# Attention in front of a routed network: a new plan for the steps of 16 units, taken by four engines in the order issued

## The chip, the cores and the metric

The kernel runs on one core of one Trainium2 chip. The metric is the device time of one execution, in microseconds (us), smaller is better. The kernel was timed in three runs; one further execution was recorded by the profiler.

## What is computed

Three networks follow each other: attention with packed queries, a layer of eight experts to which tokens are given by capacity, and a dense network. The change lies in the attention.

```
batch, n_heads, seq, head_dim = (8, 8, 576, 64)
n_pack = 32
...
def sm_attn(qq, kk, vv):
    s = scale * np.matmul(qq, kk.transpose(0, 1, 3, 2))
    s = s - np.max(s, axis=-1, keepdims=True)
    a = np.exp(s)
    a = a / (np.sum(a, axis=-1, keepdims=True) + 1e-09)
    return np.matmul(a, vv)
p_packed = sm_attn(p, k, v)
out = sm_attn(q, p_packed, p_packed)
...
x = np.ascontiguousarray(attn_out.transpose(0, 2, 1, 3)).reshape(B * S, H * D)
x = _moe_ref(x=x, **moe_kwargs)
return _moe2_ref(x=x, **moe2_kwargs)
```

First the 32 packed queries `p` of a head attend to its 576 keys and values (`p_packed`, 32 x 64), then the 576 queries `q` attend to the 32 rows of `p_packed`. The result `x` (4608 tokens x 512) goes through a gate (`x @ w_gate`), by which the experts take their tokens.

## The kernel before

The engines are TensorE (PE, its weight loads PEld), VectorE (DVE), ScalarE (ACT), GpSimd (POOL) and SyncE (SP), which issues the loads. The attention is cut into 16 units, each of four heads of one batch entry. The class `Attention` has one function for each step of a unit `u`:

- `s1_mm` (L112, PE): scores of the packed queries against the keys `kt`, into a PSUM tile `big`. `s1_max` (L118, L119, DVE): their maximum, and it times -0.125. `s1_exp` (L123, ACT): the exponential into `A`, with its sum.
- `s1_turn` (L130, PE): five transposes of `A` into another `big`. `s1_keep` (L136, L137, ACT): they are copied to `AT`. `pk_mm` (L145, PE): the product with the values `vt`, `ve`, into the one small PSUM tile `sm`.
- `pk_keep` (L151, L152, L154, DVE): one over the sum, scale and mask, into `pp`. `pk_turn` (L161, PE): two transposes into `sm`. `pk_keep2` (L167, DVE): two copies to `ppT`.
- `s2_mm` (L174, L178, PE): the product with the gate weights and the scores of the queries `qt`, into a third `big`. `s2_turn` (L184, L185, DVE): the scores turned in blocks of 32 into `w`, and the gate part copied to `Z`.
- `s2_max` (L189, DVE): row maximum. `s2_sub` (L215, POOL, three pieces): subtracted from `w`. `s2_exp` (L197, ACT): exponential of `w`. `s2_sum` (L201 to L203, DVE): row sum and its inverse. `s2_div` (L215, POOL, three pieces): `w` times the inverse. For the last unit both are one instruction on DVE (L211).
- `s2_back` (L219, DVE): `w` turned back into `A2`. `logits` (L226, PE): the unit's part of the gate logits, added up in the PSUM tile `LE` over all units.

`PLAN` gives each step a time in units, and `all_units` issues all steps of all units by the sum of the unit's number and that time:

```
def all_units(self):
    for _, u, n in sorted((u + t, u, n) for u in range(NU) for n, t in PLAN):
        getattr(self, n)(u)
```

In the kernel before, this is only the order of the program. What an engine takes first is settled by the framework's scheduler, which may put one step ahead of another on the same engine. Only from the routing on does PE have its order written out (`manual_schedule` with PE alone).

The PSUM tiles `big` are three buffers, which go round in the order of the program; `sm` is one. The loads `kt`, `vt`, `ve` and `qt` have four buffers each, and SP issues them in a fixed order (`setup`, L73 to L104): the keys and values of a unit, then the queries of the unit before. A load waits until its buffer is free.

When the last unit's logits are in `LE`, `take` copies it (L306, DVE), `load` turns it and the routing begins (L313 on). Products of `x_rows` (`px`, L242 on PE, copied to `xt` by ACT in L245, sent off by SP) make the tokens `x` from `A2` and `pp`; the first of them stand between the last logits on PE, the others between the steps of the routing.

Of the kernel before, what the change touches and what calls it, by code (L numbers as in the profile page):

```python
# [44 lines left out]
def wait(k, n):  # L45
# [1 line left out]

PLAN = [('s1_mm', 0), ('s1_max', 0.25), ('s1_exp', 1.06), ('s1_turn', 1.1), ('s1_keep', 1.5), ('pk_mm', 1.51),  # L50
        ('pk_keep', 1.7), ('pk_turn', 1.95), ('pk_keep2', 1.96), ('s2_mm', 2.25), ('s2_turn', 2.55),
        ('s2_max', 3.5), ('s2_sub', 3.65), ('s2_exp', 3.8), ('s2_sum', 3.81), ('s2_div', 4.57),
        ('s2_back', 6.15), ('logits', 6.7)]

TINY = float(np.uint32(0x380FFFFF).view(np.float32))

# [1 line left out]
class Attention:  # L58
# [172 lines left out]
# [3 lines that stand above are left out]
# [591 lines left out]
def fused_kernel(ctx: ExitStack, tc: tile.TileContext, a: dict, out: bass.AP):  # L825
# [20 lines left out]
    att = Attention(tc, a, ident, LE, xd)  # L846
# [1 line left out]
              pool(s_att, "ps_big", 3, space=PSUM), pool(s_att, "ps_sm", 1, space=PSUM))  # L848
    att.xpool = xpool
    rt = Routing(tc, a, rconst, rwk, ident, idx_all)  # L850
    att.all_units()
    le = rt.take(LE[0:96, 0:384])
    s_att.close()

# [136 lines left out]
```

## Time and profile before

| | us |
|---|---|
| median of three runs | 1525.36 (1525.34 to 1527.59) |
| the profiled execution | 1521.4 |
| span of its trace, from the first to the last instruction | 1519.4 |
| PE busy | 1436.2 (95% of the span) |
| DVE busy | 838.5 (55%) |
| ACT busy | 781.7 (51%) |
| POOL busy | 183.2 (12%) |
| mean granted clock of PE | 0.982 of full speed |

The profiled execution's time is 2.0 us more than its span. Times in the rows below are in us from the start of the span. A busy share is an average over parts of the program with quite different limits: the attention has the first 130 us or so, the routing and the experts follow, then the dense network. Matmuls are pipelined, and their ends are modelled.

### The profile page before, as it was taken

What the parts mean: (1) busy time and instruction counts of PE and PEld (TensorE: products, weight loads), DVE (VectorE), ACT (ScalarE), POOL (GpSimd) and SP (SyncE); (2) the same over time, 40 slices, a digit from 0 to 9 for tenths busy, and PEclk for the clock granted to TensorE, in tenths of its full rate; (3) what the DMA queues carried; (4) which work ended last, traced back from release to release, by engine and by line L of the source; (5) the groups of instructions that cost most, each with busy time, mean ns of one, the idle gap of its engine ahead of it and who ended that gap; (6) DMA issues with size and microseconds to landing.
All of it is one profiled execution on the core that took longest, in us unless ns stands there. A gap on an engine that the chain in (4) does not pass through costs nothing.

```text
span 1519.4 us, 22513 instructions
## 1 busy us (share of the span) xinstructions
PE 1436.2 (95%) x9009; PEld 1183.9 (78%) x9009; DVE 838.5 (55%) x1779; ACT 781.7 (51%) x966; POOL 183.2 (12%) x269
## 2 busy tenths in 40 slices
PE   6878699999999999999999999999999999999997
PEld 3335478888889899999788888888888888888885
DVE  4775588777778677543344454544445444454443
ACT  2333444433435344444656566565665656666564
POOL 2441301011010103032601010100101010010101
PEclk9999899999999999999999999999999999999999
DMA  9843636363645548452410020201002020100000
GB/s 339 304 143 126 223 131 220 120 217 127 216 141 190 171 143 307 158 179 93 158 56 28 0 83 1 83 0 56 28 1 83 1 76 7 56 28 0 28 0 28
DMA packets 66840, 165.36 MB, mean 109 GB/s; under 512 B 8880, under 2 KB 21808, under 8 KB 66736
## 3 DMA queue, kind: packets, MB, share of 16 engines
q1 hardware_dynamic: 60656, 144.00, 27.9%
q0 software_dynamic: 6080, 19.93, 3.8%
q8 instruction: 71, 1.16, 0.3%
q14 instruction: 33, 0.27, 0.1%
HBM read 117.76 MB, written 46.14 MB: 108 GB/s over the span
## 4 chain that ended last, share of the span: by engine, by line
issue 49%; PE 24%; DVE 5%; DMA 4%; POOL 3%; ACT 2%; SPq 0%; POOLq 0%; DVEq 0%; ACTq 0%
PE pm L624 18%; PE ph L624 3%; PE po L794 2%; DMA raw<-in_w 2%; POOL out L804 2%; DMA raw<-wd 2%; DVE w L547 1%; POOL w L547 1%; ACT w L540 1%; PE pt L693 1%; DVE h L715 1%; DMA xg<-xd,idx 0%; DVE dbig L585 0%; PE pr L379 0%; DVE xl L696 0%
## 5 line engine op out<-in xcount | busy, mean ns | idle before, releaser
L624 PE MATMUL ph<-y,w 128*128 128x512 f32 x1728 | 414.9, 395 | 0.0
L794 PE MATMUL po<-w,g 128*128 128x512 f32 x1728 | 410.1, 394 | 0.9 <-ACT g L769 0.9
L624 PEld LDWEIGHTS ph<-y,w 128*128 128x128 f32 x1728 | 324.1, 188 | 78.2
L794 PEld LDWEIGHTS po<-w,g 128*128 128x128 f32 x1728 | 324.9, 188 | 75.4 <-ACT g L769 1.7
L769 ACT ACTIVATE u<-u 128x1024 f32<-128x1024 f32 (+1 forms) x219 | 229.4, 1049 | 193.5 <-DVE u L773 183.2
L624 PE MATMUL pm<-h,w 128*128 128x288 f32 x1536 | 235.1, 303 | 1.8 <-DVE h L715 1.6
L624 PE MATMUL pm<-xh,w 128*128 128x288 f32 x1024 | 219.3, 304 | 0.7 <-ACT xh L695 0.7
L624 PEld LDWEIGHTS pm<-h,w 128*128 128x128 f32 x1536 | 209.7, 189 | 9.6 <-issue 3.1
L773 DVE TENSOR_SCALAR u<-ph 128x1024 f32<-128x1024 f32 (+1 forms) x73 | 88.2, 1209 | 200.4 <-PE ph L624 200.4
L769 ACT ACT_TABLE_LOAD x144 | 184.8, 1283 | 2.6
L776 DVE TENSOR_TENSOR u<-ph,u 128x1024 f32<-128x1024 f32 (+1 forms) x73 | 88.2, 1209 | 172.5 <-ACT u L769 172.5
L624 PEld LDWEIGHTS pm<-xh,w 128*128 128x128 f32 x1024 | 169.2, 192 | 8.2 <-issue 4.8
L624 PE MATMUL pm<-xl,w 128*128 128x288 f32 x512 | 156.2, 305 | 0.3 <-DVE xl L696 0.2
L778 DVE TENSOR_TENSOR u<-ph,u 128x1024 f32<-128x1024 f32 (+1 forms) x73 | 88.1, 1208 | 73.3 <-ACT u L769 73.3
L769 ACT ACTIVATE g<-u 128x1024 fp32r<-128x1024 f32 (+1 forms) x73 | 76.4, 1048 | 101.3 <-DVE u L778 93.8
L540 ACT ACTIVATE w<-raw 128x1024 fp32r<-128x1024 f32 x80 | 84.4, 1058 | 80.9 <-DMA raw<-in_w 60.6
L804 POOL DMA_INDIRECT out<-ot,idx_all x36 | 35.0, 971 | 726.8 <-DVE ot L802 721.0
L624 PEld LDWEIGHTS pm<-xl,w 128*128 128x128 f32 x512 | 98.3, 192 | 6.5 <-issue 4.4
L714 ACT ACTIVATE h<-pm 128x288 fp32r<-128x288 f32 x128 | 50.9, 405 | 90.4 <-PE pm L624 89.1
L780 DVE TENSOR_TENSOR g<-u,g 128x1024 fp32r<-128x1024 f32 (+1 forms) x73 | 88.2, 1209 | 2.7 <-ACT g L769 2.7
L683 POOL DMA_INDIRECT xg<-xd,idx x40 | 42.2, 1054 | 367.7 <-PE pr L395 186.8
L715 DVE SCALAR_TENSOR_TENSOR h<-pm,h 128x288 fp32r<-128x288 f32 x128 | 57.0, 451 | 51.2 <-ACT h L714 50.1
(160 smaller groups left out, 1133.5 us busy)
## 6 DMA issues: line engine op xcount, KB each, us to landing
raw<-in_w SPq DMA_DIRECT2D x64, 512.0 KB, 4.7
yd<-y SPq DMA_DIRECT2D x64, 288.0 KB, 3.3
kt<-in_k SPq DMA_DIRECT2D x16, 576.0 KB, 9.5
qt<-in_q SPq DMA_DIRECT2D x16, 576.0 KB, 8.8
vt<-in_v SPq DMA_DIRECT2D x16, 512.0 KB, 7.3
xd<-xt SPq DMA_DIRECT2D x32, 256.0 KB, 2.0
draw<-in_win SPq DMA_DIRECT2D x16, 512.0 KB, 4.3
wd<-dbig SPq DMA_DIRECT2D x32, 256.0 KB, 2.9
```

Source lines behind the costliest of these rows:

```text
L540: self.nc.scalar.activation(w[:, 0].rearrange("p a b -> p (a b)"), raw, AF.Copy)
L624: nc.tensor.matmul(out, l, r, start=i == 0 and m == 0, stop=i == n - 1 and m == 2)
L683: nc.gpsimd.indirect_dma_start(out=xg, out_offset=None, in_=self.xd, in_offset=bass.IndirectOffsetOnAxis(ap=idx[:, j:j + 1], axis=0))
L714: nc.scalar.activation(h[:, 0], ph, AF.Relu)
L715: nc.vector.scalar_tensor_tensor(h[:, 1], ph, 0.0, h[:, 0].bitcast(F32), op0=OP.max, op1=OP.subtract)
L769: op = nc.scalar.activation(*args, **kw)
L773: for step in (lambda p: V.tensor_scalar(u[:, p], ph[:, p], 20.0, None, op0=OP.min), lambda p: A(u[:, p], u[:, p], AF.Exp), lambda p: A(u[ ...
L776: lambda p: V.tensor_tensor(u[:, p], ph[:, p], u[:, p], op=OP.max),
L778: lambda p: V.tensor_mul(u[:, p], ph[:, p], u[:, p]),
L780: lambda p: V.tensor_sub(gt[:, 1, p], u[:, p], gt[:, 0, p].bitcast(F32))):
L794: self.nc.tensor.matmul(self.po[m], gt[:, p, i, 128 * m:128 * m + 128], self.cw[8 + f // 2][:, q, f % 2], start=f == 0 and p == q == 0, st ...
L804: st = nc.gpsimd.indirect_dma_start(out=self.out, out_offset=bass.IndirectOffsetOnAxis(ap=self.idx_all[:, c:c + 1], axis=0), in_=ot, in_of ...
```

## The change

The numbers of `PLAN` are new, and `all_units` is called with the order written out for PE, DVE, ACT and POOL: these four take the steps in the order in which the program issues them. Between two steps of a unit that hang together directly the plan now leaves 0.09 (`pk_keep2` to `s2_mm`) to 0.97 units (`s2_div` to `s2_back`), a quarter or so on average; before, some had 0.01. No step is added, removed or altered. SP isn't in the list; its order is the same in both programs, and so is DVE's from L306 on. In the changed kernel the lines of the steps are one higher (L167 becomes L168).

```
-PLAN = [('s1_mm', 0), ('s1_max', 0.25), ('s1_exp', 1.06), ('s1_turn', 1.1), ('s1_keep', 1.5), ('pk_mm', 1.51),
-        ('pk_keep', 1.7), ('pk_turn', 1.95), ('pk_keep2', 1.96), ('s2_mm', 2.25), ('s2_turn', 2.55),
-        ('s2_max', 3.5), ('s2_sub', 3.65), ('s2_exp', 3.8), ('s2_sum', 3.81), ('s2_div', 4.57),
-        ('s2_back', 6.15), ('logits', 6.7)]
+PLAN = [('s1_mm', 0.22), ('s1_max', 0.42), ('s1_exp', 0.6), ('s1_turn', 0.8), ('s1_keep', 1.0), ('pk_mm', 1.4),
+        ('pk_keep', 1.58), ('pk_turn', 1.74), ('pk_keep2', 2.01), ('s2_mm', 2.1), ('s2_turn', 2.72),
+        ('s2_max', 2.87), ('s2_sub', 3.03), ('s2_exp', 3.35), ('s2_sum', 4.09), ('s2_div', 4.33),
+        ('s2_back', 5.3), ('logits', 5.47)]
...
-    att.all_units()
+    E = mybir.EngineType
+    with tc.manual_schedule(engines={E.PE, E.DVE, E.Activation, E.Pool}):
+        att.all_units()
     le = rt.take(LE[0:96, 0:384])
```

POOL, in the middle of the attention, before (`w` with its number is one unit's tile; `x6` are the three pieces of its subtraction and the three of its division):

```order
L215 TENSOR_TENSOR w_647<-w_647,r_696 128x192 x6
L215 TENSOR_TENSOR w_722<-w_722,r_771 128x192 x6
L215 TENSOR_TENSOR w_797<-w_797,r_846 128x192 x6
L215 TENSOR_TENSOR w_872<-w_872,r_921 128x192 x6
L215 TENSOR_TENSOR w_947<-w_947,r_996 128x192 x6
```

and now:

```order
L216 TENSOR_TENSOR w_667<-w_667,r_679 128x192 x3
L216 TENSOR_TENSOR w_592<-w_592,r_604 128x192 x3
L216 TENSOR_TENSOR w_742<-w_742,r_754 128x192 x3
L216 TENSOR_TENSOR w_667<-w_667,r_679 128x192 x3
L216 TENSOR_TENSOR w_817<-w_817,r_829 128x192 x3
L216 TENSOR_TENSOR w_742<-w_742,r_754 128x192 x3
```

Before, both turns of a unit stood one behind the other; now the subtraction of the next unit (`w_742`) stands between the subtraction and the division of a unit (`w_667`).

DVE, about one unit in the middle of the attention, before:

```order
L167 COPY ppT<-sm 128x64 x2
L151 TENSOR_SCALAR mx<-mx 128x1
L219 STREAM_TRANSPOSE a_5_984<-w 128x576
L152 RECIPROCAL mx<-mx 128x1
L201 TENSOR_REDUCE r<-w 128x18
L202 TENSOR_SCALAR r<-r 128x18
L118 TENSOR_REDUCE mx<-big 128x1
L203 RECIPROCAL r<-r 128x18
L119 TENSOR_SCALAR mx<-mx 128x1
L219 STREAM_TRANSPOSE a_6_1059<-w 128x576
L184 STREAM_TRANSPOSE w<-big 128x576
```

and now:

```order
L168 COPY ppT<-sm 128x64 x2
L202 TENSOR_REDUCE r<-w 128x18
L203 TENSOR_SCALAR r<-r 128x18
L204 RECIPROCAL r<-r 128x18
L220 STREAM_TRANSPOSE a_4_855<-w 128x576
L119 TENSOR_REDUCE mx<-big 128x1
L120 TENSOR_SCALAR mx<-mx 128x1
L152 TENSOR_SCALAR mx<-mx 128x1
L153 RECIPROCAL mx<-mx 128x1
L155 SCALAR_TENSOR_TENSOR pp_814<-sm,mx,mask 128x256
L185 STREAM_TRANSPOSE w<-big 128x576
L186 COPY Z_108<-big 128x8
```

Before, the steps of several units were woven into each other and two units went differently, with two L219 in a short stretch of every second one; now every period is the same and each step is taken whole, and the new L190 closes it.

PE, about one unit in the middle of the attention, before:

```order
L161 MATMUL sm<-ident,pp_1185 128x128 x2
L112 MATMUL big<-kt,pT 64x288 x4
L130 MATMUL big<-ident,A_107 128x128 x4
L130 MATMUL big<-ident,A_107 64x128
L174 MATMUL big<-wg,ppT 64x8 x2
L178 MATMUL big<-qt,ppT 64x288 x4
L145 MATMUL sm<-vt,AT 32x64 x16
L145 MATMUL sm<-ve,AT 32x64 x4
L161 MATMUL sm<-ident,pp_1260 128x128 x2
```

and now:

```order
L162 MATMUL sm<-ident,pp_1189 128x128 x2
L131 MATMUL big<-ident,A_107 128x128 x4
L131 MATMUL big<-ident,A_107 64x128
L175 MATMUL big<-wg,ppT 64x8 x2
L179 MATMUL big<-qt,ppT 64x288 x4
L113 MATMUL big<-kt,pT 64x288 x4
L146 MATMUL sm<-vt,AT 32x64 x16
L146 MATMUL sm<-ve,AT 32x64 x4
L227 MATMUL LE<-a_9_1230,Z_111 32x384
L227 MATMUL LE<-a_9_1230,Z_111 32x192
L162 MATMUL sm<-ident,pp_1264 128x128 x2
```

Before, `s1_mm` (L112) of a unit stood behind `pk_turn` (L161) and ahead of `s1_turn` (L130) of the unit before it; now it stands behind `s2_mm` (L175, L179), and `s1_turn` (L131) is that of the same unit.

## Rows read from the trace of the kernel before

**Rows 1.** Timeline: start us, busy us, engine, line, operation, output<-inputs, count, [idle before <-releaser].

```profile
18.69 2.19 PE L112 MATMUL big<-kt,pT 128*64 128x288 f32 x8 [0.68 <-DMA kt<-in_k]
...
104.55 1.19 PE L112 MATMUL big<-kt,pT 128*64 128x288 f32 x8
...
132.56 0.55 DVE L306 COPY le<-LE 96x384 f32<-96x384 f32 x1 [2.94 <-PE LE L226]
```

**Rows 2.** Busy us by stretch: length, PE, PEld, DVE, ACT, POOL, granted clock, DMA share, GB/s.

```profile
18.69:57.36 38.67, 32.56 (x422) 16.26 (x423) 26.63 (x76) 12.35 (x29) 14.33 (x30) 0.94 1.01 372
57.36:104.54 47.18, 37.46 (x494) 18.59 (x493) 33.17 (x97) 15.30 (x35) 20.08 (x42) 0.94 0.58 209
104.54:132.56 28.02, 23.56 (x190) 12.55 (x189) 16.47 (x43) 8.90 (x17) 9.48 (x23) 0.88 0.15 52
```

**Rows 3.** DVE's waits from 18.69 to 104.54 us: total us, times, longest us.

```profile
DVE a L219 <- POOL w L215: 10.1, 6, 1.9
DVE r L201 <- ACT w L197: 6.4, 7, 1.2
```

**Rows 4.** Timeline, from the turn back of one unit to the queries' product.

```profile
96.98 0.78 DVE L219 STREAM_TRANSPOSE a<-w 128x576 f32<-128x576 f32 x1 [1.60 <-POOL w L215]
97.68 0.74 DVE L184 STREAM_TRANSPOSE w<-big 128x576 f32<-128x576 f32 x1
...
98.39 0.46 DVE L154 SCALAR_TENSOR_TENSOR pp<-sm,mx,mask 128x256 f32<-128x256 f32 x1
98.78 0.74 DVE L189 TENSOR_REDUCE r<-w 128x18 f32<-128x576 f32 x1
...
99.28 1.19 PE L112 MATMUL big<-kt,pT 128*64 128x288 f32 x8
99.44 0.34 DVE L167 COPY ppT<-sm 128x64 f32<-128x64 f32 x2
99.60 1.44 POOL L215 TENSOR_TENSOR w<-w,r 128x192 f32<-128x192 f32 x3 [2.65 <-DVE r L189]
99.70 0.14 DVE L151 TENSOR_SCALAR mx<-mx 128x1 f32<-128x1 f32 x1
99.87 0.16 DVE L152 RECIPROCAL mx<-mx 128x1 f32<-128x1 f32 x1
...
100.40 0.77 PE L130 MATMUL big<-ident,A 128*128 128x128 f32 x5
100.52 0.76 DVE L118 TENSOR_REDUCE mx<-big 128x1 f32<-128x576 f32 x1 [0.48 <-PE big L112]
...
101.10 0.29 PE L174 MATMUL big<-wg,ppT 128*64 128x8 f32 x4
...
101.24 1.17 PE L178 MATMUL big<-qt,ppT 128*64 128x288 f32 x8
```

**Rows 5.** Timeline, the copies of the last unit and the product behind them.

```profile
118.02 0.29 DVE L167 COPY ppT<-sm 128x64 f32<-128x64 f32 x2
118.24 0.40 PE L174 MATMUL big<-wg,ppT 128*64 128x8 f32 x3 [0.55 <-DVE ppT L167]
```

**Rows 6.** Timeline, the sum of the last unit on DVE.

```profile
126.75 0.75 DVE L201 TENSOR_REDUCE r<-w 128x18 f32<-128x576 f32 x1 [0.17 <-ACT w L197]
...
127.54 0.18 DVE L202 TENSOR_SCALAR r<-r 128x18 f32<-128x18 f32 x1
127.75 0.27 DVE L203 RECIPROCAL r<-r 128x18 f32<-128x18 f32 x1
```

**Rows 7.** PE's timeline behind two pauses, and two stretches with their granted clock.

```profile
70.06 1.50 PE L226 MATMUL LE<-a,Z 128*32 128x192 f32 x4 [2.03 <-DVE a L219]
...
97.81 0.84 PE L226 MATMUL LE<-a,Z 128*32 128x192 f32 x4 [2.03 <-DVE a L219]
...
70.00:72.00 2.00, 1.94 (x6) 0.48 (x6) 1.77 (x5) 0.00 (x0) 0.15 (x1) 0.50 0.99 382
...
98.00:100.00 2.00, 1.74 (x12) 0.68 (x10) 1.97 (x8) 0.00 (x0) 0.40 (x1) 1.00 0.01 4
```

## The prediction

> **What bounds the kernel now.** I read the slices of the page first, then the timeline of the first 133 us, then the waits of VectorE (DVE), then the single rows of two units. The change touches the attention alone, and its end can be found in the timeline: the copy of the gate logits `LE` (L306) starts at 132.56 us [rows 1], and the routing and all after it hang on it. From there on the order of the DVE is the same in both programs, SP's whole order is the same, and TensorE (PE) only has a few of the `px` products on other sides of the last logits. So the whole change is in when L306 starts.
>
> The attention has three parts. To 18.69 us it waits for inputs: the product of unit 2 starts when its `kt` lands [rows 1]. From there to the product of unit 15 at 104.55 us it turns its loop: 85.86 us for 13 units, 6.60 us a unit. Then 28.01 us of tail to L306 [rows 1].
>
> No engine is full in the loop. DVE is busy for 26.63 + 33.17 = 59.8 of 85.85 us, PE for 70.0, and the DMA share falls from 1.01 in the first part to 0.58 in the second [rows 2]. So order and waiting set the 6.60 us. DVE's waits say which: the turn back (L219) waits for POOL six times, 10.1 us in all, and the sum (L201) for ScalarE (ACT) seven times, 6.4 us [rows 3]. Both are one round trip: row maximum on DVE, subtraction on POOL (1.44 us), exponential on ACT, sum on DVE, division on POOL (1.44 us again), turn back on DVE. POOL had both turns of a unit directly one behind the other, so nothing lay between them and DVE stood: 1.60 us at 96.98 [rows 4].
>
> **The change part by part.** No instruction is added or removed. Moved are the steps of DVE, PE, ACT and POOL, and the moved order has POOL's subtraction of one unit ahead of the division of the unit before. What DVE asks for in these two steps is now three quarters of a unit or more behind its making: L201 of unit u-4 needs an exponential of the period before; L219 of unit u-5 needs a division of the period before. I cost both of the waits of rows 3 at nothing: POOL has 2.88 us of work a unit, against a period of 5.9 us (below), and by POOL's order the division follows a subtraction that starts at the period's beginning, so it ends some 3.4 us after it, a good 4 us ahead of its L219. If POOL were 4 us late, L219 would wait again and the loop would be at about 6.6 us as now.
>
> *What is late next in the loop.* The new DVE order of one period is L167, L201 to L203, L219, L118, L119, L151, L152, L154, L184, L185, L189; PE's is `s2_mm`, `s1_mm`, `pk_mm`, `logits`, `pk_turn`, `s1_turn`. L167 lets `s2_mm` go, `s1_mm` is queued behind that on PE, and L118 waits for `s1_mm`. Follow this ring, start to start:
> - L167 to L174 on PE: 0.22 us (118.02 to 118.24) [rows 5];
> - `s2_mm`: from 101.10 to the end of 101.24 + 1.17 is 1.31 us; PE starts the next step 0.07 us ahead of such an end (99.28 + 1.19 against 100.40), so 1.24 us [rows 4];
> - `s1_mm` to L118: 99.28 to 100.52, 1.24 us [rows 4];
> - L118 to L119: 0.79 us, as L201, as long a reduction, to its L202 [rows 6]; then L151 after 0.15, L152 after 0.17, L154 after 0.19 (its own 0.16 and 0.03) [rows 4];
> - L154 to L184: 0.39 us; L184 to L189: 0.80 us with L185 between; L189 to L167: 0.66 us [rows 4].
>
> Sum 5.85 us. Between L167 and L118 DVE has only 0.26 + 1.30 (L201, L202, L203: 0.79, 0.21, 0.27 + 0.03) + 0.70 (L219) = 2.26 us of work, less than the 2.70 us that PE needs there, so DVE waits 0.44 us a unit for L112: that is the new wait. Behind the waiting L118 stand `pk_keep`, `s2_turn` and `s2_max` on DVE, and they are in the sum. DVE's own steps come to 5.41 us. So the loop is bounded by 5.41 from below and by 6.60 from above (nothing gained), and I take 5.85, since it is a sum of measured steps: 13 x 5.85 = 76.1 us, **9.8 us gained**.
>
> *Loads.* One unit brings 1728 KB (`kt` and `qt` 576 KB each, `vt` 512, half a `ve`), 1.77 MB. At the 372 GB/s of the full queue [rows 2] that is 4.8 us, under 5.85. The buffers come free at the same steps, four units deep, and SP's order is unchanged, so I cost the loads at nothing; if they were short by a unit, one period would stretch by under 4.8 us.
>
> *Start.* Now `s1_turn` of unit 0 and `pk_mm`, `pk_turn`, `s1_turn` and `s2_mm` of units 0 and 1 stand ahead of `s1_mm` of unit 2, which came right at 18.69 before. PE was at the low level of its clock in part of this: the product of unit 2 took 2.19 us against 1.19 later [rows 1, 4]. At full speed those steps end before `kt` lands (cost 0); at half speed I find some 2 us. I take 1.0 us **lost**.
>
> *Tail.* After `s1_mm` of unit 15 DVE is the one that works through: 1.24 to L118, 3.15 to L167 of unit 14 (the steps above), then a round without L118: 0.26 + 1.30 + 0.70 + 0.17 + 0.19 + 0.39 + 0.80 + 0.66 = 4.5; a round without `pk_keep` but with unit 15's subtraction on DVE: 0.26 + 1.30 + 0.70 + 0.80 + 0.77 + 0.70 = 4.5; then two sums, three turns back and the last division: 2 x 1.30 + 2 x 0.70 + 0.79 + 0.78 = 5.6; then the logits of unit 15, 0.84 and 0.1 to L306 [rows 7]. That is 19.9 us. PE has six and a half `px` tiles in front of the last logits; today's L306 waits 2.94 us [rows 1], 2.0 of it for such tiles. Bounds 0 to 4 us, and I take 1.5, a little under today's. So 21.4 us against 28.01: **6.6 us gained**. The tail now has only 16.47 us of DVE work in 28 us [rows 2], which is where this comes from.
>
> Sum: -1.0 + 9.8 + 6.6 = **15.4 us**. Behind L306 a chain from DVE to PE and back follows, with nothing in it that is bound to a fixed time, so I carry it to the end in full. The profiled execution took 1521.4 us: 1506.0. The median of the three runs, 1525.36, stands 4.0 us (0.26%) above it, so the forecast for a median is **1510 us**.
>
> A rule against going by the ring: the Trainium skill, "Perfetto Trace Analysis", section "Identifying the Most-Contended Engine", has the engine of the highest occupancy set what is to be won. By it DVE's own 5.41 us would be the loop's period, 5.7 us better than my sum; the waits of rows 3 show that this loop isn't bounded by occupancy, and I go by the ring.
>
> **The rivals.**
> 1. *PE's clock takes part of it.* PE's 2.48 us in the ring are new on the path, and they double at the low level. Two pauses of 2.03 us of the same kind were followed once by products of 1.50 us, with a granted clock of 0.50 in the stretch 70 to 72 us, and once by 0.84 us, with 1.00 at 98 to 100 [rows 7]. The new loop leaves PE 5.85 - 5.1 = 0.75 us of pause a unit in all (the 5.1 is worked out in the next rival), which speaks against falls; the start and the tail have longer pauses. A stretch of low clock of one to four periods and a slow tail cost 2.5 us each time: 4 to 12 us of the gain are gone, 1514 to 1522.
> 2. *The other side: PE falls to the low level and stays there.* PE's busy 70.0 us over 13 units at a mean clock of 0.94 [rows 2] are 5.1 us a unit at the full level, 10.1 at the low one. Were the whole loop low, it would take 13 x 10.1 = 131 us, 45 us more than now, less the 5.6 us of start and tail: about 1565. It decides from the point where half of the periods are low (13 x 2.48 x 0.48 = 15.4). For it speaks that the clock does fall in today's loop, to a mean of 0.94; against it, that PE's pauses get shorter. The Trainium skill, "TensorE: Matmul & The Clock Gate", section "HAM oscillation", tells of loops where bursts of products and waits alternate and the clock falls back each time, which would give this case; the row at 97.81 speaks against it.
> 3. *DVE alone sets the loop.* If the queued PE steps overlap more than I count, the period is 5.41 us: 5.7 us more, 1504; with no `px` tiles in the way 1503 or a little less.
> 4. *The gain does not arrive.* Some part of the routing might wait for something that was late anyway, or the round trip might stay bound at 6.6 us (the change would then not do what it says): 1525. Against the first: the DMA share is 0.15 in the tail [rows 2].
>
> **How the numbers follow.** A measurement of this kernel tells about 0.2% (3 us) from no change. Forecast (1505 to 1514): 0.70. Rival 1: 0.13, nearly all of it still faster by over 3 us. Rival 3: 0.08. Rival 4: 0.05. Rival 2: 0.04. Faster: 0.70 + 0.13 + 0.08 = 0.91; same 0.05; slower 0.04. For the range I take the forecast's own, rival 3 down to 1503 and rival 1 up to 1520, which leaves out rivals 2 and 4, the end of rival 1, and the far end of rival 3.
>
> **What would show it.** In the profile after, the products L112 (then a line further down) of unit 3 to unit 15 should start every 5.8 to 5.9 us and evenly, where they now alternate; DVE's waits for POOL at the turn back and for ACT at the sum should be near nothing in the loop, and its wait for the product at the maximum some 0.4 us a unit. L306 should start at about 117 us. I am wrong in the ring if the period is under 5.6 or over 6.1 us; wrong on the clock if a granted 0.5 shows up between 30 and 95 us; wrong on carrying if L306 is 15 us earlier and the end is not.

## The result and the profile after

The changed kernel takes 1509.86 us (median of four runs, 1506.34 to 1511.4), the kernel before beside it 1525.98 us (four runs). The ratio on record is 0.9883, with a 95% interval from 0.9864 to 0.9901: 1.17% faster (the bare quotient of the two medians is 0.9894; the ratios below are taken from the record in the same way). The forecast was 1510.0. The profiled execution took 1506.34 us, the shortest of the four; its forecast was 1506.0.

The timeline of the changed kernel shows the marks of the prediction (lines are one higher than before; columns as in [rows 1]):

```profile
18.42 1.19 PE L113 MATMUL big<-kt,pT 128*64 128x288 f32 x8 [0.68 <-DMA kt<-in_k]
...
30.17 1.24 PE L113 MATMUL big<-kt,pT 128*64 128x288 f32 x8
...
37.10 1.73 PE L113 MATMUL big<-kt,pT 128*64 128x288 f32 x8
...
43.48 1.24 PE L113 MATMUL big<-kt,pT 128*64 128x288 f32 x8
...
84.77 1.24 PE L113 MATMUL big<-kt,pT 128*64 128x288 f32 x8
...
96.56 1.24 PE L113 MATMUL big<-kt,pT 128*64 128x288 f32 x8
...
114.95 1.56 PE L243 MATMUL px<-pp,a 128*128 128x256 f32 x6
...
116.44 0.84 PE L227 MATMUL LE<-a,Z 128*32 128x192 f32 x4
...
117.32 0.55 DVE L307 COPY le<-LE 96x384 f32<-96x384 f32 x1 [2.24 <-PE LE L227]
```

These are units 2, 4, 5, 6, 13 and 15, then the last `px` products and the last logits ahead of the copy, and the copy of the gate logits. That copy stood at 132.56 [rows 1] and now starts at 117.32, 15.24 us earlier. The span is 1504.6 us against 1519.4, 14.8 us shorter, so nearly all of it arrives. From unit 12 (78.86, in the period below) to unit 13 are 5.91 us.

The same stretches as in [rows 2] (loop and tail), and 107.44 us behind the copy, in the windows of the changed kernel (columns as there):

```profile
18.42:96.56 78.14, 63.92 (x912) 44.32 (x913) 63.19 (x176) 28.77 (x64) 34.44 (x72) 0.98 0.85 312
96.56:117.32 20.76, 18.26 (x175) 10.08 (x171) 17.19 (x42) 7.67 (x14) 9.60 (x23) 1.00 0.17 58
117.32:224.76 107.44, 89.60 (x699) 67.47 (x700) 72.08 (x276) 46.26 (x76) 17.59 (x24) 0.90 0.50 169
```

And the stretch behind the copy in the kernel before:

```profile
132.56:240.00 107.44, 88.92 (x697) 66.92 (x698) 72.28 (x276) 45.71 (x75) 17.94 (x24) 0.90 0.49 167
```

Behind the copy the busy times of the two agree to within a microsecond on each engine, so what follows the attention was shifted and did not change. The loop is 78.14 us instead of 85.86, the tail 20.76 instead of 28.01.

DVE's waits in the loop, from 18.42 to 96.56 us, after (total us, times, longest us):

```profile
DVE mx L119 <- PE big L113: 13.9, 13, 3.3
```

It is the only line. Both waits of [rows 3], 16.5 us together, are gone. The wait for the product at the maximum is left, and it isn't wholly new. In the kernel before, in the window of [rows 3], it stood in third place:

```profile
DVE mx L118 <- PE big L112: 6.3, 6, 2.5
```

It has grown from 6.3 to 13.9 us and now comes in every unit (its longest, 3.3 us, is that for the `kt` of unit 2 at the start). The granted clock of the loop rose from 0.94 [rows 2] to 0.98, but that isn't the gain: where it is 1.00 in both, two units take 13.49 us before (85.79 to 99.28) and 11.79 us now (84.77 to 96.56).

One period of the loop, in the timeline after, from the copies of `ppT` of one unit to those of the next:

```profile
77.44 0.35 DVE L168 COPY ppT<-sm 128x64 f32<-128x64 f32 x2
77.60 2.94 POOL L216 TENSOR_TENSOR w<-w,r 128x192 f32<-128x192 f32 x6 [2.96 <-DVE r L190]
77.70 0.74 DVE L202 TENSOR_REDUCE r<-w 128x18 f32<-128x576 f32 x1
77.71 0.35 PE L175 MATMUL big<-wg,ppT 128*64 128x8 f32 x3 [0.63 <-DVE ppT L168]
...
78.86 1.24 PE L113 MATMUL big<-kt,pT 128*64 128x288 f32 x8
78.87 0.72 DVE L220 STREAM_TRANSPOSE a<-w 128x576 f32<-128x576 f32 x1
...
80.15 0.76 DVE L119 TENSOR_REDUCE mx<-big 128x1 f32<-128x576 f32 x1 [0.56 <-PE big L113]
...
83.33 0.35 DVE L168 COPY ppT<-sm 128x64 f32<-128x64 f32 x2
```

The ring of the prediction can be read off by starts: 0.27 us from L168 to L175, 1.15 to L113, 1.29 to L119, 3.18 to the next L168; sum 5.89. DVE is ready 0.56 us ahead of the product and stands. L202 and L220 carry no wait, and POOL does its two turns (x6) behind one wait.

### The profile page after: what moved, and what is told of

Same layout as the page of the kernel before. It is cut to its first block, busy times and chain, and to the rows that moved or that the text cites. A ratio compares the mean times of both kernels' runs of the same rounds, so it can differ in the third digit from the quotient of the medians.

```text
span 1504.6 us, 22525 instructions
## 1 busy us (share of the span) xinstructions
PE 1426.7 (95%) x9009; PEld 1191.8 (79%) x9009; DVE 841.5 (56%) x1779; ACT 783.0 (52%) x966; POOL 183.5 (12%) x269
## 3 DMA queue, kind: packets, MB, share of 16 engines
q8 instruction: 71, 1.16, 0.3%
## 4 chain that ended last, share of the span: by engine, by line
issue 46%; PE 24%; DVE 7%; DMA 6%; POOL 3%; ACT 2%; SPq 0%; POOLq 0%; DVEq 0%; ACTq 0%
PE pm L625 17%; DMA raw<-in_w 4%; PE ph L625 3%; PE po L795 2%; DVE w L548 2%; POOL out L805 2%; DMA raw<-wd 1%; ACT w L541 1%; POOL w L548 1%; DVE h L716 1%; PE pt L694 1%; DVE dt L585 0%; PE pr L380 0%; DVE dbig L586 0%; DVE ge L372 0%
```

## The experiments

The start of the gate-logits copy is quoted with each run, because it measures the attention alone. What lies behind it took 1386.5 to 1390.2 us in the changed kernel, its second run, e2, e3 and e8, but 1383.7 to 1399.9 us in the others, more than some of the effects looked for.

### e1: the new plan, order not written out

```
-    E = mybir.EngineType
-    with tc.manual_schedule(engines={E.PE, E.DVE, E.Activation, E.Pool}):
-        att.all_units()
+    att.all_units()
```

> The new plan without the written-out order: the framework's scheduler settles the engines' order again. Theory A (plan and written-out order belong together; the scheduler weaves the steps by estimates of its own, so the three quarters of a unit between exponential and sum don't survive): the loop has uneven units again, mean over 6.2 us, and the time is within 10 us of the kernel before (1516 to 1536). Rival B (the new numbers alone do it): the loop at 5.9 us and about 1510.

Measured: 1530.76 us (five runs), ratio to the kernel before 1.005 (1.0027 to 1.0072), so half a per cent slower. Loop 95.65 us, 7.36 a unit; the copy at 140.74. DVE's waits from 24 to 90 us:

```profile
DVE a L220 <- POOL w L216: 10.9, 8, 1.6
DVE r L202 <- ACT w L198: 7.4, 9, 1.2
```

The two waits of [rows 3] are back. What follows: the table alone gains nothing. What the framework's scheduler made of it has DVE wait for the round trip again.

### e2: the old plan, order written out

```
-PLAN = [('s1_mm', 0.22), ('s1_max', 0.42), ...
+PLAN = [('s1_mm', 0), ('s1_max', 0.25), ...
```

The four engines keep the written-out order of the change; all numbers of the table are those of before.

> The old plan with the written-out order of the four engines. The old plan has the division of a unit (4.57) ahead of the next unit's subtraction (4.65), so the round trip from maximum to sum stays on DVE's path: from L190 the sum can start 0.83 + 1.47 + 0.04 + 0.68 + 0.04 = 3.06 us later, and DVE has 2.3 us of other steps between them (a turn, a pk_keep, the maximum itself). Theory A: DVE waits some 0.75 us a unit for ACT at the sum, which on its own steps of 5.25 us makes about 6.0 us a unit; even units; with a longer tail (the plan is 6.7 units deep instead of 5.5) some 1512 to 1518. Rival C (the written-out order alone does it all): 1510 or less, without waits for ACT at the sum.

Measured: 1512.6 us (eight runs), ratio 0.9951 (0.9928 to 0.9974). The copy starts at 122.91, the tail is 27.4 us. The loop takes 76.5 us, in its steady part 5.91 a unit. One period in the timeline of e2:

```profile
72.14 0.75 DVE L201 TENSOR_REDUCE r<-w 128x18 f32<-128x576 f32 x1 [0.69 <-ACT w L197]
...
73.53 0.77 DVE L219 STREAM_TRANSPOSE a<-w 128x576 f32<-128x576 f32 x1
...
75.04 0.74 DVE L189 TENSOR_REDUCE r<-w 128x18 f32<-128x576 f32 x1
...
75.87 1.44 POOL L215 TENSOR_TENSOR w<-w,r 128x192 f32<-128x192 f32 x3 [0.87 <-DVE r L189]
...
77.34 0.68 ACT L197 ACTIVATE w<-w 128x576 f32<-128x576 f32 x1 [2.79 <-POOL w L215]
```

Here another ring is closed: 2.90 us of DVE's order from L201 of one unit to L189 of a later one, 0.83 to POOL's subtraction, 1.47 to the exponential, and 0.71 (a little more than its 0.68) to the next L201, which waits for it: 5.91. That the new plan's ring comes to the same period is a coincidence of two sums. What follows: writing the order out is by itself enough for the gain in the loop. On POOL e2 has the order of before: by the old numbers the division of a unit still comes next behind its subtraction. Even so the turn back (L219 at 73.53) no longer waits for POOL, so POOL's order alone didn't make that wait. Before, L219 came to DVE right behind the division it needs (POOL ends at 95.50 + 1.44, L219 starts at 96.98 [rows 4]); in the order of the table it comes 1.58 units behind it (6.15 against 4.57). The other wait, for ACT at the sum, is still there in every unit (0.69 us at 72.14) and is part of e2's ring; only with the numbers of the change is it gone. They also give the shorter tail (20.76 against 27.4), by which the copy comes 5.6 us earlier in the changed kernel than in e2.

### e3: the round trip without its three quarters of a unit

```
-        ... ('s2_sum', 4.09), ('s2_div', 4.33),
-        ('s2_back', 5.3), ('logits', 5.47)]
+        ... ('s2_sum', 3.4), ('s2_div', 3.45),
+        ('s2_back', 4.3), ('logits', 4.47)]
```

> The changed kernel with s2_sum at 3.4, s2_div at 3.45, s2_back at 4.3 and logits at 4.47: on POOL the division of a unit stands ahead of the next unit's subtraction again, all else as in the changed kernel, order written out and every unit alike. Theory A: the round trip is back on DVE's path: 3.06 us from L190 to the sum, 1.17 us for the sum's three instructions, 2.51 us from L119 to the next L190: 6.74 us a unit, against 5.90; 13 x 0.84 = 11 us more in the loop, less up to 4 us of a shallower tail: 1515 to 1523; DVE waits for ACT at L202 every unit, above 1 us. Rival D (what counts is that every unit is alike, not where POOL's turns stand): 5.9 us a unit and about 1510.

Measured: 1517.44 us (nine runs), ratio 0.9973 (0.9958 to 0.9987). The loop turns every 6.65 us, the tail is 22.4 us, the copy at 126.61. DVE's timeline:

```profile
76.42 0.77 DVE L220 STREAM_TRANSPOSE a<-w 128x576 f32<-128x576 f32 x1
78.51 0.75 DVE L202 TENSOR_REDUCE r<-w 128x18 f32<-128x576 f32 x1 [1.32 <-ACT w L198]
```

What follows: the new table needs its slack around the sum and the division; without it a wait for ACT of 1.32 us returns every unit, and the loop is at the 6.6 us of before. POOL has the same order in e2 and in e3, with 5.91 and 6.65 us a unit. So that order alone doesn't set the period; what the new order on POOL is worth by itself no run here shows.

### e4: the product of the next unit ahead of `s2_mm`

```
-PLAN = [('s1_mm', 0.22), ('s1_max', 0.42), ...
+PLAN = [('s1_mm', 0.05), ('s1_max', 0.42), ...
```

This cuts the ring at one place: on PE, L113 no longer stands behind L175, so it doesn't wait for the copies L168.

> The changed kernel with s1_mm at 0.05 instead of 0.22: on PE s1_mm of unit u stands ahead of s2_mm of unit u-2, so L119 no longer waits for a product that is queued behind one that waits for L168. Theory A (the ring L168, s2_mm, s1_mm, L119 sets 5.90 us): the ring is broken, DVE's wait at L119 goes to nearly nothing and DVE's own steps set the unit: 5.25 us by the rows of the changed kernel; 13 x 0.65 = 8.4 us less: about 1501. Rival E (PE's own work, 5.1 us and more where the clock is low, or the loads, 4.8 us, bound it next to the ring): 5.5 to 5.9 us a unit, 1505 to 1510.

Measured: 1494.84 us (five runs), ratio 0.9831 (0.981 to 0.9852). The copy starts at 108.07. The loop's window and, behind it, DVE's timeline from L202 of one unit to that of the next:

```profile
17.98:86.13 68.15, 61.97 (x911) 35.59 (x912) 60.07 (x171) 27.93 (x62) 33.17 (x69) 1.00 0.97 359
```

```profile
71.16 0.75 DVE L202 TENSOR_REDUCE r<-w 128x18 f32<-128x576 f32 x1
...
72.97 0.72 DVE L119 TENSOR_REDUCE mx<-big 128x1 f32<-128x576 f32 x1
...
76.38 0.74 DVE L202 TENSOR_REDUCE r<-w 128x18 f32<-128x576 f32 x1
```

No row of it has a wait; 5.22 us a unit are DVE's own steps from start to start, and DVE is busy for 60.07 of 68.15 us. What follows: the ring was the bound of the changed kernel, and DVE is the next one. The loads are close behind it, with a DMA share of 0.97 in this window.

### e5 and e6: the change again, and e4 with a load moved

The kernel e5 is the changed kernel, unaltered, beside the runs that follow. The kernel e6 is e4 with the second part of `pT` loaded later:

```
-        nc.sync.dma_start(self.pT[:, 8:], a["pT"][:, 8:])
         for u in range(2, NU):
...
                 self.load(w, n)
+                if (n, u) == ("v", 2):
+                    nc.sync.dma_start(self.pT[:, 8:], a["pT"][:, 8:])
```

> The changed kernel, unaltered, next to the ones of this call. Theory A: loop at 5.90 us a unit, L307 about 117 us, ratio to before 0.986 to 0.991. A spell of low clock between 30 and 40 us (one period was 6.9 us long in the first profile) may or may not come again; without it the loop is 76.7 us, with it 78.

> s1_mm at 0.05 as in e4_s1first, and the large last part of pT (768 KB, needed from unit 4 on) loaded behind the inputs of unit 2 instead of ahead of them. Theory A (unit 2 starts when its kt lands): 786 KB at 385 GB/s are 2.0 us; the other steps ahead of unit 2's product end at about 16.4 us, so it starts 1.5 to 2 us earlier, at 16 to 16.5, and L307 comes at 106 to 106.6 instead of 108.1: 1.5 to 2 us less than e4_s1first. Rival F (the start hides behind something else, such as the low clock): no gain.

Measured: e5 1510.32 us (six runs), ratio 0.9915 (0.9892 to 0.9938), copy at 116.95. e6 1500.36 us (five runs), ratio 0.9839 (0.9815 to 0.9863), copy at 107.38. In this comparison on one chip the intervals lie apart, so the kernel e6, with `s1_mm` at 0.05 and the moved load, is faster than the change as well as than the kernel before. For the moved load itself the run is a miss: the copy came 0.7 us earlier than in e4, not 1.5 to 2. PE's timeline in e6 says why:

```profile
16.37 0.71 PE L132 MATMUL big<-ident,A 128*128 128x128 f32 x5
17.01 1.19 PE L114 MATMUL big<-kt,pT 128*64 128x288 f32 x8
...
23.60 1.19 PE L114 MATMUL big<-kt,pT 128*64 128x288 f32 x8 [1.89 <-DMA kt<-in_k]
```

Unit 2 starts right behind PE's own transposes, with no wait for `kt`: 0.97 us earlier than in e4, and there PE's order became the bound. Part of that is lost again, since the moved load now stands ahead of the `kt` of unit 3: units 3 and 4 wait for their `kt` (1.89 and 0.30 us), and unit 4 starts only 0.7 us earlier than in e4 (28.59 against 29.29). That is the 0.7 us of the copy. What lies behind the copy was 10 us longer in e6 than in e4. I have no cause for that and only one profile of each: of its five executions e4's profile is the shortest, e6's the longest.

### e7: the `px` products held behind the last logits

This is e4 with PE's written-out order in one piece from the attention into the routing, so that no `px` stands ahead of the last logits:

```
-    with tc.manual_schedule(engines={E.PE, E.DVE, E.Activation, E.Pool}):
+    pe_order = ExitStack()
+    pe_order.enter_context(tc.manual_schedule(engines={E.PE}))
+    with tc.manual_schedule(engines={E.DVE, E.Activation, E.Pool}):
         att.all_units()
...
-    with tc.manual_schedule(engines={mybir.EngineType.PE}):
+    with pe_order:
```

> s1_mm at 0.05 as in e4_s1first, and PE's order written out in one piece from the attention to the routing, so that no px product stands ahead of the last logits: all 12 px tiles that PE now has before the first product of the search (L380) stand between L314 and it. Theory A (tail: the px tiles cost L307 about 1.4 of its 2.25 us of waiting, but are worth more than they cost, since ACT empties them at 0.7 us each): L307 1.2 to 1.5 us earlier, but L380 comes 8.5 to 9 us after L314 instead of 5.2: 2 to 2.5 us more in all. Rival G (the px tiles in front of the last logits are a plain loss): 1.3 us less.

Measured: 1508.75 us (four runs), ratio 0.9899 (0.9875 to 0.9923) where e4 has 0.9831, some 10 us slower, with a copy at 107.30, 0.8 us earlier. PE's windows in e7 (columns as in [rows 2]), then its timeline:

```profile
96.00:102.00 6.00, 2.27 (x16) 1.07 (x16) 5.83 (x15) 1.36 (x2) 3.04 (x7) 1.00 0.00 0
...
104.00:106.00 2.00, 1.69 (x6) 0.38 (x8) 1.68 (x3) 0.00 (x0) 0.00 (x0) 0.50 0.00 0
...
108.00:110.00 2.00, 2.00 (x7) 1.73 (x8) 1.25 (x5) 0.00 (x0) 0.00 (x0) 0.50 0.00 0
```

```profile
102.39 0.83 PE L227 MATMUL LE<-a,Z 128*32 128x384 f32 x4 [3.21 <-DVE a L220]
104.31 2.95 PE L227 MATMUL LE<-a,Z 128*32 128x192 f32 x8 [1.09 <-DVE a L220]
...
108.44 13.92 PE L243 MATMUL px<-pp,a 128*128 128x256 f32 x48
122.29 0.34 PE L380 MATMUL pr<-ge,oh 128*32 128x128 f16 x9
```

The same product of the routing in e4, with the `px` products ahead of it:

```profile
109.18 4.42 PE L243 MATMUL px<-pp,a 128*128 128x256 f32 x18
114.10 0.33 PE L380 MATMUL pr<-ge,oh 128*32 128x128 f16 x9 [0.50 <-DVE ge L372]
```

Without the `px` products PE has 2.27 us of work in 6, pauses for 3.21 us, and its granted clock falls to 0.50 (in e4 it is 1.00 in every 2 us from 92 to 116). The last two logits take 2.95 us. L380 starts 15.0 us behind the copy instead of 6.0, mostly because 48 `px` products now stand between copy and L380, where e4 has 18: at e4's 0.245 us each (4.42 / 18), the 30 more come to some 7.4 us, an estimate. The 48 at that rate would be 11.8 us and took 13.92, so the low level (0.50 still at 108 to 110) cost some 2 us more. What follows: the `px` ahead of the last logits delay the copy by a little (0.8 us here), and without them the clock fell; the direction was foreseen, the size was not. The expectation had each of the twelve tiles (four products) at ACT's 0.7 us, and e4's rate is nearly 1.0 us.

### e8: three buffers for the loads

```
-    att.setup(long, pool(s_att, "short"), pool(s_att, "ld", 4), pool(s_att, "awk", 4),
+    att.setup(long, pool(s_att, "short"), pool(s_att, "ld", 3), pool(s_att, "awk", 4),
```

> The changed kernel with three buffers for each of the loads instead of four. Theory A (loads cost nothing: a unit's 1.77 MB need 4.7 us of its 5.9, and a load has two periods and more of cover): 5.90 us a unit and the time of the changed kernel within 2 us. Rival H (the loads run just in time, and their cover is needed): waits of PE for DMA in the loop, more than 6 us a unit.

Measured: 1511.86 us (four runs), ratio 0.9915 (0.9888 to 0.9941), the same as e5. Period 5.90. PE's waits from 18 to 97 us in e8:

```profile
PE big L175 <- DVE ppT L168: 8.1, 13, 0.6
PE sm L162 <- DVE pp L155: 6.1, 13, 1.1
```

No load is among them, so even with a buffer less the loads cost nothing in the loop. The copy came at 118.76, since unit 2 started at 19.81, 1.4 us later than in the changed kernel. That was no load either: PE's own step ahead of it, in e8, took 2.15 us, where the changed kernel has 1.17 (at 16.57):

```profile
17.86 2.15 PE L179 MATMUL big<-qt,ppT 128*64 128x288 f32 x8
```

## Why the prediction was right, and where its terms were off

The time, the place and the new wait came as forecast. Of the terms two were too pessimistic and one too optimistic, and their errors cancel: +0.3 + 7.7 + 7.25 = 15.25 us against -1.0 + 9.8 + 6.6 = 15.4. That the sum came within 0.2 us is luck; the terms were off by 0.65 to 2.1 us.

- **Loop, right in its mechanism.** The ring was put at 5.85 us a unit and is 5.89 by the rows above, 2.71 of it on PE (forecast 2.70) and 3.18 on DVE (3.15). DVE's wait is 0.56 us, not 0.44, and "the new wait" is an old one that grew (6.3 us in the loop before). Rows 4 don't show the 0.80 us from L184 to L189, as L154 stands between them there; the changed kernel has 0.80 (99.55 to 100.35). e4 cuts the ring and the loop falls to 5.22; e3 shows that the slack at the sum is needed; e8 that the loads aren't the bound.
- **Loop, the size.** 7.7 us were gained, not 9.8 (85.86 - 78.14). 0.6 of the missing 2.1 us is 13 times the 0.045 us a unit by which the steady period, 5.895 us, is longer than 5.85. The other 1.5 is a spell of low clock: unit 5's and 6's periods are 6.93 and 6.38 us instead of twice 5.90, and the product with `qt`, which is in the ring, took nearly twice its time in it (2.16 us at 35.27, in the last section, against 1.16 at 42.59). The prediction named a granted 0.5 between 30 and 95 us as what would make it wrong on the clock, and there is one, once. It is rival 1 in small: the rival's 2.5 us was meant for a period that is wholly low. What spoke against it, 0.75 us of pause a unit, was a mean over the whole loop; ahead of the spell, where no logits run yet, PE paused for 1.06 and 0.62 us in one unit.
- **Loop, what was credited.** "I cost both of the waits of rows 3 at nothing", because POOL's turns had new slack: both waits are gone with the new plan. But the 6.60 us of before is not only the old plan's doing. By e2 the old plan in written-out order also turns in 5.91 us, held by a ring the prediction didn't look for, and by e1 the new plan without written-out order is slower than before. The step that failed is the one that put the old waits down to POOL's two turns standing one behind the other. That order is the same in e2: there the wait for POOL is gone, so it came from the order that the scheduler made of the plan, and the wait for ACT at the sum stays (0.69 us a unit), so that one the old numbers bring with them.
- **Start.** It was put at 1.0 us lost, between 0 and some 2. It cost nothing: unit 2 came at 18.42 (before 18.69), still waiting for its `kt`, and its product took 1.19 us where it had taken 2.19 [rows 1]. PE had more to do ahead of it and was through in time, as its steps there went at full speed (16.57: 1.17 us). That was not sure to come: in e8 the same steps went at half speed, and unit 2 came 1.4 us later, which is the case that the prediction put at some 2 us. The granted clock doesn't tell the two cases apart, as it is on record as 1.00 from 14 to 18 us in both; here the durations do.
- **Tail.** 7.25 us gained, 6.6 forecast. The wait for `px` ahead of the copy was taken as 1.5 us. The last logits began at 116.44 and the copy 0.88 us later, so of the copy's 2.24 us of wait (DVE was through at 115.08) 1.36 were that (the `px` at 114.95 stood ahead). The rest of the difference, 0.5 us, is DVE's steps. e2 gives the same gain from the other side: with the old numbers the tail stays at 27.4 us.
- **Carrying.** Forecast in full, and the two windows behind the copy are alike; 14.8 of 15.24 us are in the span.
- **The rivals.** Rival 2 (PE low throughout) falls: the mean granted clock of the loop is 0.98. Rival 3's bound (DVE alone, forecast 5.41, in e4 5.22) is real, and wasn't reached because the ring stood in front of it. Rival 4 falls: it arrived.

Not settled is why the rest of the program differs by several microseconds between kernels that have the same order there, as e6 and e4 do.

## What to carry to other kernels

In a loop that goes round several engines which each take their steps in a fixed order, look for the ring: follow a step from its engine to the next and back to itself by starts. The longest such sum set the period here (5.89 us in the changed kernel, 5.91 in e2), though no engine in it was full. A table of issue times does only what the engines' order lets it do, so write the order out, or read what the scheduler made of it, before crediting the numbers. When a ring is found, move the one step that closes it (here `s1_mm` ahead of `s2_mm`): that brought the copy another 9.2 us forward (117.32 to 108.07).

## What the runs showed of the hardware that was not expected

The granted clock fell with short pauses only. The windows of the changed kernel from 32 to 38 us:

```profile
32.00:34.00 2.00, 0.94 (x14) 0.78 (x15) 1.83 (x8) 0.83 (x2) 0.00 (x0) 1.00 1.04 420
34.00:36.00 2.00, 1.38 (x11) 0.98 (x11) 1.93 (x6) 0.75 (x2) 1.20 (x3) 0.69 1.04 306
36.00:38.00 2.00, 2.00 (x10) 1.45 (x9) 0.79 (x2) 0.69 (x1) 1.69 (x4) 0.50 1.02 354
```

And PE's pauses ahead of it, with a product in it:

```profile
33.30 0.44 PE L162 MATMUL sm<-ident,pp 128*128 128x128 f32 x2 [1.06 <-DVE pp L155]
...
34.91 0.41 PE L175 MATMUL big<-wg,ppT 128*64 128x8 f32 x3 [0.62 <-DVE ppT L168]
...
35.27 2.16 PE L179 MATMUL big<-qt,ppT 128*64 128x288 f32 x7
```

The clock went from 1.00 to 0.50 behind pauses of 1.06 and 0.62 us, where one of 2.03 us had once gone without a fall [rows 7], so the length of a single pause doesn't tell it. Nor do the two pauses as such: the unit before had the same work of PE (busy 0.94 and 1.38 of 2 us from 26 to 30 us) and kept 1.00. From 39.59 us on the first logits fill part of the first pause, and no fall follows in the loop. PE's waits in the changed kernel from 42 to 96 us:

```profile
PE big L175 <- DVE ppT L168: 6.2, 10, 0.6
PE sm L162 <- DVE pp L155: 2.6, 9, 0.3
```

In e5 the same spell came one unit earlier (0.51 from 30 to 32 us) and in e8 it came too (0.50 from 38 to 40 us), each time once. The logits needn't be what ends it: in e5 the clock was back at 1.00 from 32 us on, and its first logits came at 39.24. Why it comes once and not again stays open. The Trainium skill, "TensorE: Matmul & The Clock Gate", section "A second HAM failure mode: psum-queue depth-cycling", tells of a kernel whose TensorE rests briefly but often between groups of products and goes up and down between its levels. This trace agrees with that only for the one spell: from 42 to 96 us PE still pauses in every period, for 0.3 and 0.6 us, and its level stays up.
